# Fused retention attention and two MLPs on one core: first visits of 3, 7, 13 and 9 slices, and low parts a step later

## Chip, cores and metric

The kernel runs on one core of one Trainium2 chip. The metric is device time in microseconds of one execution; the kernel before has a median of 1159.39 us over three runs (1157.38 to 1161.65).

## What is computed

A linear attention with a decay for each head, and two pairs of dense layers behind it, the first with a leaky ReLU, the second with an ELU. Queries, keys and values are float32; **the weights are float64**.

```python
for t in range(S):                       # B 4, H 8, S 768, D 64
    state = gamma[None, :, None, None] * state + np.einsum('bhd,bhe->bhde', k[:, :, t], v[:, :, t])
    y[:, :, t] = scale * np.einsum('bhd,bhde->bhe', q[:, :, t], state)
x = y.transpose(0, 2, 1, 3).reshape(3072, 512)
h = x @ moe_w_in;  g = np.maximum(0.01 * h, h);  x = g @ moe_w_out      # 512 -> 2048 -> 512
h = x @ moe2_w_in; g = np.where(h > 0, h, np.exp(np.minimum(h, 0)) - 1); out = g @ moe2_w_out
```

## The kernel before

**Products.** Every operand of the dense layers is held as two float32r parts, high and low, and each product is three matmuls: high by high, high by low, low by high. Tokens go in six blocks of 512, the inner size of 2048 in 16 slices of 128. A **step** is one block with one slice: `gemm1` (L254) makes `h` with 12 matmuls, the first two of each three with the high part of the weights and the third with the low part; ACT makes `gf` (`leaky`, L343) and its high part `ghi`, DVE the low part `glo` (`split_g`, L266); `gemm2` (L273) then adds 12 matmuls into the four banks `y`. `drain` (L299) issues the gemm2 of the steps up to a given one, and at the end of a visit it evacuates `y` (two copies on DVE, two on ACT) to DRAM, or adds an earlier part.

**Weights.** A slice of first-phase weights comes in as raw 64-bit words, one MB for both of its matrices (`load`, L86, on SP's queue), and is turned into high and low parts on the chip, in place. The operations are listed once, in order, by `conv_ops` (L182): put (ACT takes the exponent words out), exp (two mask operations on DVE, then a bias on ACT), top, low and sign on DVE, mul on DVE with the copy w to the high part on ACT behind it, and split on DVE, the low part. The put of the next piece is issued between a piece's sign and its mul; the split of a piece comes after the exp of the next. The first slices are taken in halves (a: `w_in`, b: `w_out`), the others whole. `conv(n)` (L198) issues the next n of these, puts not counted, **as long as the piece at the head of the list has been asked for by `load`**; `need` (L211) issues as many as it takes to have a given slice ready.

**Order.** All engines work through their instructions in program order, and the program's order is written out by hand. First come chunks 0 to 7 of the attention (128 tokens each, for blocks 0 and 1; L483): for each, the scores of the next chunk, `prep` on POOL, the chunk's outputs, the next chunk's mask (`pt`, DVE), then one conversion operation, the new state and the low part of x, and one more conversion operation. Three pairs of PSUM banks rotate among scores and outputs. Then comes `plan` (L505), a list of (step, drain up to this step, operations before, operations after). An entry issues gemm1, `conv(n1)`, `gf`, `ghi` and `glo`, the drain, `conv(n2)` and possibly one `load_w`. Blocks 0 and 1 take turns in the first entries, so that one converted slice serves two steps; `VISITS` (L48) says how many slices each visit has. The other 16 chunks are spread over the steps (`out_at`, `sc_at`). The second phase takes its weights from DRAM, where the first phase's last visits leave them converted.

**Space.** Each slice has its tile `w0` to `w15`. Before raw words are put there, the upper ones hold the chunks' keys, queries and values (`kv`, chunk c in `w{15-c}`), the staged `y` of first visits (`w15`), and the `g` of steps that wait long for their gemm2 (`wait`, in `w14` and `w13`). A load into such a tile waits until it is free.

Of the kernel before, what the change touches and what calls it, by code (L numbers as in the profile page):

```python
# [20 lines left out]
F32 = mybir.dt.float32  # L21
F32R = mybir.dt.float32r
# [5 lines left out]
ALU = mybir.AluOpType  # L28
# [4 lines left out]
P = 128  # L33
C = 128
NT = B * S
NCB = S // C
NCH = B * NCB
NP = H // 2
BLK = 512
CPB = BLK // C  # L40
NB = NT // BLK
KD = DM // P
MF = DFF // P
HM = MF // 2
V0 = 4


VISITS = (  # L48
    [(0, 0, V0), (1, 0, HM), (0, V0, MF), (1, HM, MF)] + [(j, 0, MF) for j in range(2, NB)],
    [(j, 0, MF) for j in range(NB)],  # L50
)

# [2 lines left out]
def body(ctx: ExitStack, tc: tile.TileContext, kkv, w1, w2, tabs, out):  # L55
    nc = tc.nc
    big = ctx.enter_context(tc.tile_pool(name="big", bufs=1))
    wp = ctx.enter_context(tc.tile_pool(name="wp", bufs=1))
    cv = ctx.enter_context(tc.tile_pool(name="cv", bufs=2))
    gp = ctx.enter_context(tc.tile_pool(name="gp", bufs=2))  # L60
# [8 lines left out]
    xhi = [big.tile([P, KD, BLK], F32R, name=f"xhi{b}") for b in range(2)]  # L69
    xlo = [big.tile([P, KD, BLK], F32R, name=f"xlo{b}") for b in range(2)]  # L70
# [5 lines left out]
    nload = nload2 = 0  # L76


    halves = [(0, 0), (1, 0), (0, 1), (2, 0), (1, 1), (3, 0), (2, 1), (3, 1)]
    pieces = [(m, a, 1) for m, a in halves] + [(m, 0, 2) for m in range(V0, MF)]  # L80
    loaded = set()

# [15 lines left out]
    def load_w2():  # L98

        nonlocal nload2  # L100
        m = nload2
        for a in range(2) if m < V0 else (0,):
            n = 1 if m < V0 else 2
            t = place(m, a, n, F32R, "w")
# [91 lines left out]
    queue = list(conv_ops())  # L196

    def conv(n):  # L198

        while queue and queue[0][1][:2] in loaded:  # L200
            op, i = queue[0]
            if op is not c_put:
                if not n:
                    break
                n -= 1
            queue.pop(0)
            op(i)
            while exps:
                bias(exps.pop(0))
# [56 lines left out]
    def split_g(s, gf, eng, pool, bufs):  # L266
        ghi = pool.tile([P, BLK], F32R, tag="ghi", name="ghi", bufs=bufs)
        glo = pool.tile([P, BLK], F32R, tag="glo", name="glo", bufs=bufs)
        nc.scalar.copy(ghi, gf)  # L269
        eng.tensor_tensor(glo, gf, ghi.bitcast(F32), ALU.subtract)  # L270
        g[s] = ghi, glo
# [16 lines left out]
    acc, g = None, {}  # L288
# [54 lines left out]
    def leaky(h):  # L343
        gf = gp.tile([P, BLK], F32, tag="gf", name="gf", bufs=2)
        nc.scalar.activation(gf, h, AF.Prelu, alpha=0.01)  # L345
        return gf


    with ExitStack() as actx:
# [12 lines left out]
        def att_load(c, first=0, last=4):  # L362

            if first == 0:
                if c < 2 * CPB:
                    kv[c] = wp.tile([P, 4, DM], F32, tag=f"w{MF - 1 - c}", name="kv")
                else:
                    kv[c] = ap_.tile([P, 4, DM], F32, tag="kv", name="kv")
            nc.sync.dma_start(out=kv[c][:, first:last, :], in_=kkv[c, :, first:last, :])
# [31 lines left out]
        def outputs(c, pool, tag):  # L401


            cb = c % NCB
            t = pt.pop(c)
            o = pool.tile([P, 2, BLK], F32, tag=tag, name="o")
            places = [(i, k, 2 * i + k, r) for i in range(2) for k in range(2) for r in range(2)]
            by_column = [(i, k, 2 * i + k, x ^ k) for i in range(2) for k in range(2) for x in range(2)]
            for i, k, a, r in by_column:
                v = kv[c][:, 3, a * C + r * D : a * C + (r + 1) * D]  # L410
                nc.tensor.matmul(o[half(r ^ k), k, pair(i)], v, t[:, r, pair(a)], start=(i == 0), stop=True, skip_group_check=True)  # L411
            if cb < NCB - 1:
                for i, k, a, r in places:
                    hs = slice(a * C + r * D, a * C + (r + 1) * D)
                    nc.tensor.matmul(o[half(r), k, 2 * C + i * D : 2 * C + (i + 1) * D], kv[c][:, 2, hs], kv[c][:, 3, hs],  # L415
                                     start=False, stop=True, skip_group_check=True)
            if cb:
                for i, k, a, r in places:
                    nc.tensor.matmul(o[half(r ^ k), k, pair(i)], st[half(r), 2 * k + i, :], kv[c][half(r), 1, pair(a)],  # L419
                                     start=False, stop=True, skip_group_check=True)  # L420
            b, ts = c // CPB % 2, slice(c % CPB * C, (c % CPB + 1) * C)
            x = [z[b][:, :, ts].rearrange("p (k i) t -> p k i t", k=2) for z in (xhi, xlo)]
            y = o[:, :, : 2 * C].rearrange("p k (i t) -> p k i t", i=2)
            nc.scalar.copy(x[0], y)
            return o, x, y

        def states(c, o, x, y):
            cb = c % NCB
            if cb < NCB - 1:
                n = st.rearrange("p (k i) d -> p k (i d)", k=2)  # L430
                m = sg.rearrange("p (k i) d -> p k (i d)", k=2)
                if cb:
                    nc.vector.tensor_tensor(n, m, o[:, :, 2 * C : 2 * C + 2 * D], ALU.add)
                else:
                    nc.vector.tensor_copy(n, o[:, :, 2 * C : 2 * C + 2 * D])
            nc.vector.tensor_tensor(x[1], y, x[0].bitcast(F32), ALU.subtract)
            if cb < NCB - 2:
                nc.vector.tensor_tensor(sg, st, gtab.unsqueeze(2).to_broadcast([P, NP, D]), ALU.mult)

        def prep(c):  # L440
# [12 lines left out]
        for x in halves[2:]:  # L453
            load(*x, 1)
        nload = V0
        for _ in range(2):
            load_w()

        def warm(n):
# [10 lines left out]
        banks = itertools.cycle(((ps, "y0"), (ps, "y1"), (aps, "x")))  # L470

        def early_masked(c, sc):
            masked(c, sc, *((wp, "w7") if c % 2 else (ap_, "pt")))

        early_masked(0, scores(0, *next(banks)))
        o = outputs(0, *next(banks))
        warm(1)
        states(0, *o)
        sc = scores(1, *next(banks))
        prep(1)  # L480
        warm(1)
# [1 line left out]
        for c in range(1, 2 * CPB):  # L483
            if c + 1 < 2 * CPB:
                sc = scores(c + 1, *next(banks))
                prep(c + 1)
            o = outputs(c, *next(banks))
            if c + 1 < 2 * CPB:
                early_masked(c + 1, sc)
            conv(1)  # L490
            states(c, *o)
            conv(1)


        out_at, sc_at = {}, {}
# [5 lines left out]
        NA = next(s for s, (_, j, _, _) in enumerate(steps) if j == NB - 1)  # L501

        plan = [(0, -1, 2, 2), (4, -1, 2, 2), (1, 0, 4, 3), (5, 0, 2, 2), (2, 1, 4, 3), (6, 1, 2, 2), (3, 3, 2, 3), (7, 5, 3, 5)]  # L505
        plan += [(s, s - 2, 3 if s < 12 else 2, 3 if s == 8 else 2) for s in range(8, NA)]
        wait = [wp.tile([P, 4, BLK], F32R, tag=f"w{MF - 2 - i}", name="gx") for i in range(2)]
        for n, (s, upto, n1, n2) in enumerate(plan):
            ph, j, m, (_, _, m0, m1, vi) = steps[s]
            h = (aps if n % 2 else ps).tile([P, BLK], F32, tag="z" if n % 2 else "h", name="h")  # L510
            gemm1(0, m, j % 2, h)
            conv(n1)
            gf = leaky(h)
            c = out_at.get(s)
            if c is not None:
                o = outputs(c, aps, "x")
                states(c, *o)
                if c < NCH - 2:
                    att_load(c + 2)
            if 4 <= s < 8:  # L520
                i = 2 * (s % 2)
                ghi, glo = g[s] = [wait[s // 2 - 2][:, i + k, :] for k in range(2)]
                nc.scalar.copy(ghi, gf)
                nc.vector.tensor_tensor(glo, gf, ghi.bitcast(F32), ALU.subtract)
            else:
                split_g(s, gf, nc.vector, gp, 3)
            drain(upto, stage_w if vi < 2 or m < m0 + 2 and vi == 2 else stage_f)
            c = sc_at.get(s)
            if c is not None:
                sc = scores(c, aps, "x")  # L530
                prep(c)
                masked(c, sc, ap_, "pt")
            conv(n2)
            if s in (8, 9):
                att_load(2 * CPB + s - 8)
            if nload < (MF - 1 if s > 11 else MF - 3) or vi > 1 and m > m0 + 1:
                load_w()
            if vi > 3:

                if m == 2 and npre < 2 * MF:  # L540
                    pre_load()
                if 2 < m < MF - 1:
                    pre(m < MF - 2)
            if m0 > 0 and m == m1 - 3:
                need(MF - 1, 1)
                reload(0, j, stage_f)


    with ExitStack() as ectx:
# [44 lines left out]
        for s in range(NA, 2 * NS):  # L594
# [6 lines left out]
            if ph == 0:  # L601
                gf = leaky(h)
# [10 lines left out]
            if (ph, vi) in comes:  # L613
                nx, i = comes[ph, vi], m // 2
# [68 lines left out]
```

## Time and profile before

| | |
|---|---|
| median of three runs | 1159.39 us |
| the profiled execution | 1159.4 us, its span 1157.6 us |
| PE busy | 1138.3 us of the span |
| DVE, ACT, POOL busy | 653.2, 542.2 and 93.2 us |
| mean granted TensorE clock | 0.995 |
| HBM read, written | 84.68 and 31.46 MB |

The span runs from the first to the last instruction of the profiled execution. Busy times are sums over an engine's instructions. Matmuls are pipelined, so one of them lasts longer (0.39 us) than the distance to the next (0.227 us); a group of 12 is best read from start to start. A timeline row's bracket says how long the engine stood idle ahead of it and what released it. A line number can be that of a helper: L176 is every split, L172 every w, L270 every `glo`.

### The profile page before, as it was taken

The page shows a single profiled execution, that of the slowest core. Times are in us where ns is not written, and L with a number is a line of the kernel's source. Part 1 is how long each engine was busy: PE and PEld are TensorE (multiplying, and loading weights), DVE is VectorE, ACT ScalarE, POOL GpSimd, SP SyncE. Part 2 cuts the span into 40 slices and gives each one's busy share as a digit, 9 for nine tenths or more (in the row PEclk, how much of TensorE's full clock was granted, in tenths as well). Part 3 has the DMA queues.
Part 4 walks back from the last instruction along what each step waited for, and adds up shares of the span by engine and source line. Part 5 has one row for each costly group of instructions (what it writes and reads, how often), then busy time and mean ns, then how long its engine had stood idle before and what let it go on. Part 6 is the DMA issues. An engine that isn't in the chain of part 4 may idle for free.

```text
span 1157.6 us, 14906 instructions
## 1 busy us (share of the span) xinstructions
PE 1138.3 (98%) x6024; PEld 930.9 (80%) x6024; DVE 653.2 (56%) x1049; ACT 542.2 (47%) x901; POOL 93.2 (8%) x77
## 2 busy tenths in 40 slices
PE   8989999999999999999999999999999999999998
PEld 6767788788888888888888888888888888888886
DVE  5879773235654564651212666666666666766655
ACT  2555552224444443441323654654654655555553
POOL 4000001102221222220000000000000000000000
PEclk9989999999999999999999999999999999999999
DMA  9931303334554554430645400100100100000000
GB/s 377 377 129 54 109 21 116 115 115 154 193 200 154 193 195 151 161 131 1 218 183 196 148 19 1 55 19 1 55 19 1 55 19 1 37 1 1 37 1 37
DMA packets 29877, 117.10 MB, mean 101 GB/s; under 512 B 3312, under 2 KB 3312, under 8 KB 23792
## 3 DMA queue, kind: packets, MB, share of 16 engines
q1 hardware_dynamic: 29808, 116.15, 27.4%
q8 instruction: 47, 0.77, 0.3%
q14 instruction: 22, 0.18, 0.1%
HBM read 84.68 MB, written 31.46 MB: 100 GB/s over the span
## 4 chain that ended last, share of the span: by engine, by line
PE 89%; DVE 4%; ACT 2%; issue 0%; ACTq 0%; DVEq 0%
PE y L286 43%; PE h L263 42%; PE sc L393 2%; PE o L411 1%; DVE f L134 1%; DVE f L127 1%; PE o L419 1%; ACT w L172 1%; PE o L415 1%; ACT e L120 0%; DVE glo L270 0%; DVE e L131 0%; DVE f L123 0%; DVE w L176 0%; ACT gf L345 0%; ACT ghi L269 0%
## 5 line engine op out<-in xcount | busy, mean ns | idle before, releaser
L263 PE MATMUL h<-xhi,w 128*128 128x512 f32 x1536 | 506.2, 391 | 1.8 <-DVE w L176 1.2
L270 DVE TENSOR_TENSOR glo<-gf,ghi 128x512 fp32r<-128x512 f32 x188 | 131.0, 697 | 375.6 <-ACT ghi L269 373.6
L263 PEld LDWEIGHTS h<-xhi,w 128*128 128x128 f32 x1536 | 288.0, 188 | 65.6 <-DVE w L176 2.5
L263 PE MATMUL h<-xlo,w 128*128 128x512 f32 x768 | 299.0, 389 | 0.0
L286 PE MATMUL y<-ghi,w 128*128 128x512 f32 x736 | 247.3, 398 | 5.7 <-DVE w L176 2.4
L286 PE MATMUL y<-w,ghi 128*128 128x512 f32 x768 | 236.5, 389 | 0.0
L286 PEld LDWEIGHTS y<-ghi,w 128*128 128x128 f32 x736 | 140.1, 191 | 38.6 <-DVE w L176 2.9
L286 PEld LDWEIGHTS y<-w,ghi 128*128 128x128 f32 x768 | 144.1, 188 | 29.9
L263 PEld LDWEIGHTS h<-xlo,w 128*128 128x128 f32 x768 | 144.3, 188 | 29.5
L572 ACT ACTIVATE n<-h 128x512 f32<-128x512 f32 x96 | 57.4, 598 | 224.3 <-PE h L263 224.3
L286 PE MATMUL y<-w,glo 128*128 128x512 f32 x384 | 149.4, 389 | 0.0
L286 PE MATMUL y<-glo,w 128*128 128x512 f32 x368 | 144.7, 393 | 0.0
L345 ACT ACTIVATE gf<-h 128x512 f32<-128x512 f32 x96 | 56.9, 593 | 164.4 <-PE h L263 164.1
L269 ACT CAST ghi<-gf 128x512 fp32r<-128x512 f32 x188 | 115.3, 613 | 5.8 <-DVE gf L583 3.4
L286 PEld LDWEIGHTS y<-w,glo 128*128 128x128 f32 x384 | 72.1, 188 | 15.0
L286 PEld LDWEIGHTS y<-glo,w 128*128 128x128 f32 x368 | 70.3, 191 | 14.4
L580 DVE SCALAR_TENSOR_TENSOR a<-n,a 128x512 f32<-128x512 f32 x96 | 65.6, 684 | 5.9 <-ACT n L575 5.9
L582 DVE SCALAR_TENSOR_TENSOR t<-a,t 128x512 f32<-128x512 f32 x96 | 66.4, 692 | 3.3
L583 DVE SCALAR_TENSOR_TENSOR gf<-h,t 128x512 f32<-128x512 f32 x96 | 66.4, 691 | 3.3
L120 ACT ACTIVATE e<-e,ebias 128x512 int16<-128x512 uint16 (+1 forms) x52 | 42.7, 821 | 50.9 <-DVE e L117 50.9
L581 DVE SCALAR_TENSOR_TENSOR t<-n,t 128x512 f32<-128x512 f32 x96 | 65.7, 685 | 0.0
L573 ACT ACTIVATE t<-n 128x512 f32<-128x512 f32 x96 | 60.7, 632 | 3.1
(51 smaller groups left out, 806.3 us busy)
## 6 DMA issues: line engine op xcount, KB each, us to landing
kv<-in_kkv SPq DMA_DIRECT2D x23, 1024.0 KB, 6.2
raw<-in_w SPq DMA_DIRECT2D x40, 512.0 KB, 3.8
wscr<-raw SPq DMA_DIRECT2D x32, 512.0 KB, 2.6
raw<-in_w SPq DMA_DIRECT2D x12, 1024.0 KB, 11.5
w<-wscr SPq DMA_DIRECT2D x12, 1024.0 KB, 4.7
xs<-yscr SPq DMA_DIRECT2D x12, 512.0 KB, 3.7
out<-osb SPq DMA_DIRECT2D x24, 256.0 KB, 2.9
yscr<-ysb SPq DMA_DIRECT2D x16, 256.0 KB, 2.8
```

Of the source, the lines that this page charges most:

```text
L120: nc.scalar.activation(e.bitcast(I16), e, AF.Relu, bias=ebias, scale=2.0**3)
L263: nc.tensor.matmul(h, a, x, start=(n == 0), stop=(n == 3 * KD - 1))
L269: nc.scalar.copy(ghi, gf)
L270: eng.tensor_tensor(glo, gf, ghi.bitcast(F32), ALU.subtract)
L286: nc.tensor.matmul(acc[d], lhsT, rhs, start=(first and n == 0), stop=(last and n == 2))
L345: nc.scalar.activation(gf, h, AF.Prelu, alpha=0.01)
L572: nc.scalar.activation(n, h, AF.Relu, scale=-1.0)
L573: nc.scalar.activation(t, n, AF.Tanh, scale=-0.5)
L580: nc.vector.scalar_tensor_tensor(out=a, in0=n, scalar=1.0, in1=a, op0=ALU.add, op1=ALU.mult)
L581: nc.vector.scalar_tensor_tensor(out=t, in0=n, scalar=1.0, in1=t, op0=ALU.add, op1=ALU.mult)
L582: nc.vector.scalar_tensor_tensor(out=t, in0=a, scalar=2.0, in1=t, op0=ALU.add, op1=ALU.mult)
L583: nc.vector.scalar_tensor_tensor(out=gf, in0=h, scalar=0.0, in1=t, op0=ALU.max, op1=ALU.add)
```

## The change

The first visits have 3 and 7 slices where they had 4 and 8 (`V0, V1 = 3, 7`), so slices 0 to 2 come in halves, and seven slices are used by both blocks in turn. `plan` is written anew. The `g` of eight steps (3, 4, 5, 10 to 13) waits in four tiles, `w14` down to `w11`, where four steps' waited in two. Three slices are asked for ahead of the plan, then one for each entry up to 11 slices; the other five are asked for from entry 16 on. `glo` is written in the next entry, behind its `conv(n1)`, unless the drain of its own entry wants it or nothing is left to convert. In the attention, DVE's new state comes ahead of ACT's copy of the output, and the low part of x (with the decayed state) an iteration later in the first eight chunks, behind the next mask. In chunks 4 to 7 one conversion operation is issued and not two.

```diff
-HM = MF // 2
-V0 = 4
+V0, V1 = 3, 7
-    [(0, 0, V0), (1, 0, HM), (0, V0, MF), (1, HM, MF)] + [(j, 0, MF) for j in range(2, NB)],
+    [(0, 0, V0), (1, 0, V1), (0, V0, MF), (1, V1, MF)] + [(j, 0, MF) for j in range(2, NB)],
...
-    halves = [(0, 0), (1, 0), (0, 1), (2, 0), (1, 1), (3, 0), (2, 1), (3, 1)]
+    halves = [(0, 0), (1, 0), (0, 1), (2, 0), (1, 1), (2, 1)]
...
-            nc.scalar.copy(x[0], y)
-            return o, x, y
-
-        def states(c, o, x, y):
+            return o
+
+        def states(c, o):
...
                     nc.vector.tensor_copy(n, o[:, :, 2 * C : 2 * C + 2 * D])
+            x, y = halves_of(c, o)
+            nc.scalar.copy(x[0], y)
...
+        def lows(c, o):
+
+            x, y = halves_of(c, o)
             nc.vector.tensor_tensor(x[1], y, x[0].bitcast(F32), ALU.subtract)
-            if cb < NCB - 2:
+            if c % NCB < NCB - 2:
                 nc.vector.tensor_tensor(sg, st, gtab.unsqueeze(2).to_broadcast([P, NP, D]), ALU.mult)
...
-        for _ in range(2):
+        for _ in range(3):
             load_w()
...
-            o = outputs(c, *next(banks))
+            before, o = o, outputs(c, *next(banks))
             if c + 1 < 2 * CPB:
                 early_masked(c + 1, sc)
+            lows(c - 1, before)
             conv(1)
-            states(c, *o)
-            conv(1)
+            states(c, o)
+            if c < CPB:
+                conv(1)
+        lows(c, o)
...
-        plan = [(0, -1, 2, 2), (4, -1, 2, 2), (1, 0, 4, 3), (5, 0, 2, 2), (2, 1, 4, 3), (6, 1, 2, 2), (3, 3, 2, 3), (7, 5, 3, 5)]
-        plan += [(s, s - 2, 3 if s < 12 else 2, 3 if s == 8 else 2) for s in range(8, NA)]
-        wait = [wp.tile([P, 4, BLK], F32R, tag=f"w{MF - 2 - i}", name="gx") for i in range(2)]
+        plan = [(0, -1, 2, 2), (3, -1, 2, 2), (1, 0, 2, 4), (4, 0, 2, 2), (2, 1, 3, 3), (5, 5, 0, 5)]
+        plan += [(6, 5, 2, 2), (10, 5, 2, 2), (7, 6, 2, 3), (11, 6, 2, 2), (8, 7, 2, 3), (12, 7, 2, 2), (9, 9, 1, 4), (13, 12, 3, 6)]
+        plan += [(s, s - 2, 3, 2) for s in range(14, NA)]
+        later = {}
+        for k, (m, ss) in enumerate(((MF - 2, (3, 4)), (MF - 3, (5,)), (MF - 4, (10, 11)), (MF - 5, (12, 13)))):
+            t = wp.tile([P, 4, BLK], F32R, tag=f"w{m}", name="gx")
+            later.update({x: (t[:, 2 * i, :], t[:, 2 * i + 1, :]) for i, x in enumerate(ss)})
+        lows_due = []
+
+        def g_lows():
+            while lows_due:
+                s, gf = lows_due.pop()
+                nc.vector.tensor_tensor(g[s][1], gf, g[s][0].bitcast(F32), ALU.subtract)
+
         for n, (s, upto, n1, n2) in enumerate(plan):
...
             conv(n1)
+            g_lows()
             gf = leaky(h)
...
+            nc.scalar.copy(g[s][0], gf)
+            lows_due.append((s, gf))
+            if not queue or s <= upto:
+                g_lows()
...
-            if s in (8, 9):
-                att_load(2 * CPB + s - 8)
-            if nload < (MF - 1 if s > 11 else MF - 3) or vi > 1 and m > m0 + 1:
+            if s in (14, 15):
+                att_load(2 * CPB + s - 14)
+            if nload < (MF if n > 15 else MF - 5):
                 load_w()
```

## Rows read from the trace of the kernel before

**Rows 1.** The page's first part: busy us (share of the span) and instructions.
```profile
PE 1138.3 (98%) x6024; PEld 930.9 (80%) x6024; DVE 653.2 (56%) x1049; ACT 542.2 (47%) x901; POOL 93.2 (8%) x77
```

**Rows 2.** Busy time by stretch: columns named in the first line.
```profile
core 0: us, PE busy (x) PEld busy (x) DVE busy (x) ACT busy (x) POOL busy (x), PEclk, DMA share, GB/s
...
28.00:38.30 10.30, 6.89 (x136) 5.77 (x133) 10.23 (x18) 3.55 (x6) 2.85 (x2) 1.00 1.02 422
...
68.05:76.00 7.95, 7.95 (x22) 6.34 (x23) 5.05 (x10) 2.51 (x4) 0.00 (x0) 0.62 0.01 2
...
90.00:102.50 12.50, 11.54 (x49) 8.42 (x47) 11.66 (x17) 7.91 (x11) 0.00 (x0) 1.00 0.22 84
...
122.50:129.30 6.80, 4.62 (x14) 3.57 (x14) 5.98 (x9) 4.38 (x7) 0.00 (x0) 0.75 0.69 201
```

**Rows 3.** Timeline of PE: start us, us, instruction; in brackets idle before, and releaser.
```profile
36.24 1.09 PE L411 MATMUL o<-pt,kv 128*64 128x128 f32 x16 [1.59 <-DVE pt L399]
...
38.33 0.50 PE L263 MATMUL h<-xhi,w 128*128 128x512 f32 x1
...
64.89 0.50 PE L286 MATMUL y<-ghi,w 128*128 128x512 f32 x1 [1.14 <-ACT w L172]
...
68.05 1.22 PE L286 MATMUL y<-ghi,w 128*128 128x512 f32 x2 [2.42 <-DVE w L176]
...
124.81 0.47 PE L286 MATMUL y<-ghi,w 128*128 128x512 f32 x1 [2.18 <-DVE ysb L320]
...
129.22 0.40 PE L263 MATMUL h<-xhi,w 128*128 128x512 f32 x1
...
183.83 0.67 PE L419 MATMUL o<-kv,st 64*64 64x128 f32 x16
```

**Rows 4.** Chain that ended last, in order of time: start us, us.
```profile
132.13 2.72 PE y L286 x12
```

**Rows 5.** Timeline of DVE, then of POOL, in the first chunks.
```profile
26.91 1.13 DVE L116 TENSOR_SCALAR s<-e 128x512 uint16<-128x512 uint16 x1
...
29.41 1.22 DVE L176 TENSOR_TENSOR w<-f,w 128x512 fp32r<-128x512 f32 x1
...
29.05 1.05 POOL L375 TENSOR_TENSOR kv<-kv,tab 128x512 f32<-128x512 f32 x1 [1.16 <-DMA kv<-in_kkv]
```

**Rows 6.** Timeline of DVE: one half piece, from split to split.
```profile
49.52 0.69 DVE L176 TENSOR_TENSOR w<-f,w 128x512 fp32r<-128x512 f32 x1 [0.16 <-ACT w L172]
...
51.28 0.69 DVE L270 TENSOR_TENSOR glo<-gf,ghi 128x512 fp32r<-128x512 f32 x1 [0.74 <-ACT ghi L269]
...
54.33 0.69 DVE L176 TENSOR_TENSOR w<-f,w 128x512 fp32r<-128x512 f32 x1 [0.16 <-ACT w L172]
```

**Rows 7.** Timeline of DVE: one whole slice, from split to split.
```profile
95.80 1.22 DVE L176 TENSOR_TENSOR w<-f,w 128x1024 fp32r<-128x1024 f32 x1 [0.32 <-ACT w L172]
...
98.80 0.69 DVE L270 TENSOR_TENSOR glo<-gf,ghi 128x512 fp32r<-128x512 f32 x1
...
102.46 1.23 DVE L176 TENSOR_TENSOR w<-f,w 128x1024 fp32r<-128x1024 f32 x1 [0.32 <-ACT w L172]
```

**Rows 8.** Timeline of ACT: `gf`, `ghi`, a put, the next; and a w.
```profile
65.38 0.58 ACT L345 ACTIVATE gf<-h 128x512 f32<-128x512 f32 x1
66.05 0.62 ACT L523 CAST gx<-gf 128x512 fp32r<-128x512 f32 x1
66.57 1.11 ACT L113 COPY e<-raw 128x1024 int16<-128x1024 int16 x1
67.58 0.59 ACT L345 ACTIVATE gf<-h 128x512 f32<-128x512 f32 x1
...
101.38 1.05 ACT L172 CAST w<-f 128x1024 fp32r<-128x1024 f32 x1 [2.40 <-DVE f L134]
```

**Rows 9.** DMA issues in 95 to 103 us: KB each, median us to landing.
```profile
raw<-in_w SPq DMA_DIRECT2D x1, 1024.0 KB, 4.7
```

**Rows 10.** Timeline of DVE: the state of the first later chunk.
```profile
185.19 0.42 DVE L433 TENSOR_TENSOR st<-sg,o 128x256 f32<-128x256 f32 x1 [4.45 <-ACT xhi L424]
```

More of the change, by code (lines that the diff above doesn't have):

```diff
@@ L420, in outputs @@
                                      start=False, stop=True, skip_group_check=True)
-            b, ts = c // CPB % 2, slice(c % CPB * C, (c % CPB + 1) * C)
-            x = [z[b][:, :, ts].rearrange("p (k i) t -> p k i t", k=2) for z in (xhi, xlo)]
-            y = o[:, :, : 2 * C].rearrange("p k (i t) -> p k i t", i=2)
-            nc.scalar.copy(x[0], y)
-            return o, x, y
-        def states(c, o, x, y):
+            return o
+        def states(c, o):
             cb = c % NCB
@@ L435, in states, with halves_of @@
                     nc.vector.tensor_copy(n, o[:, :, 2 * C : 2 * C + 2 * D])
+            x, y = halves_of(c, o)
+            nc.scalar.copy(x[0], y)
+        def halves_of(c, o):
+            b, ts = c // CPB % 2, slice(c % CPB * C, (c % CPB + 1) * C)
+            x = [z[b][:, :, ts].rearrange("p (k i) t -> p k i t", k=2) for z in (xhi, xlo)]
+            return x, o[:, :, : 2 * C].rearrange("p k (i t) -> p k i t", i=2)
+        def lows(c, o):
+            x, y = halves_of(c, o)
             nc.vector.tensor_tensor(x[1], y, x[0].bitcast(F32), ALU.subtract)
-            if cb < NCB - 2:
+            if c % NCB < NCB - 2:
                 nc.vector.tensor_tensor(sg, st, gtab.unsqueeze(2).to_broadcast([P, NP, D]), ALU.mult)
@@ L477, in body @@
         warm(1)
-        states(0, *o)
+        states(0, o)
         sc = scores(1, *next(banks))
@@ L516, in body @@
                 o = outputs(c, aps, "x")
-                states(c, *o)
+                states(c, o)
+                lows(c, o)
                 if c < NCH - 2:
                     att_load(c + 2)
[L520 to L524, printed above, removed]
-            else:
-                split_g(s, gf, nc.vector, gp, 3)
+            if s in later:
+                g[s] = later[s]
+            else:
+                g[s] = [gp.tile([P, BLK], F32R, tag=x, name=x, bufs=3) for x in ("ghi", "glo")]
+            nc.scalar.copy(g[s][0], gf)
+            lows_due.append((s, gf))
+            if not queue or s <= upto:
+                g_lows()
             drain(upto, stage_w if vi < 2 or m < m0 + 2 and vi == 2 else stage_f)
```

## The prediction, made before the changed kernel was run

> **What bounds the kernel now.** I read the page's engine busy times first, then the chain that ended last, then busy time by stretch, and last the timelines of PE, DVE and ACT over the first 180 us. PE is busy for 98% of the span [rows 1], and from about 130 us on the chain is matmul groups end to end, 2.72 us for each group of 12 [rows 4]; the change leaves that part's matmuls as they are. What can move is the start and the stretch in which the weights are converted. Call the gemm1 of a step g1, its gemm2 g2, and T0 the start of the first g1: 38.33 us [rows 3]. From T0 to 129.22 us PE runs 28 such groups, 76.2 us of work, in 90.9 us: **14.7 us are lost**. They lie in three places. The first is the wait for the output half of slice 2 (64.9 to 68.05, with 1.14 and 2.42 us idle) and the slow clock behind it: at a granted 0.62, 22 matmuls take 7.95 us instead of 5.0 [rows 2, 3]; about 7.6 in all. The second is three waits for `w L176` from 90 to 106 us, about 1 us each, where the clock stays at full speed, 2.9 in all [rows 2]. The third is the first visit's evacuation, 2.18 us idle and again a slow clock, 4.0 in all [rows 2, 3]. Behind all three stands DVE, in part because it waits in every step for ACT's `ghi` before it can write `glo` (0.74 us in the row) [rows 6]. Before T0, in 28 to 38.3 us, DVE is full (10.23 of 10.3) and PE works 6.9 of 10.3 us [rows 2].
>
> **The start.** Chunk 7's outputs wait for its `pt` on DVE, which sits behind everything DVE was given before [rows 3]. Ahead of that `pt` now stand two conversion operations fewer (low and sign of m1a) and one low part of x fewer (chunk 5's); at about 0.6 us each, 0.8 for the sign, that is 2.0 us. Not all of it arrives: the bank in which chunk 7's scores are put is now freed by the low part of chunk 4, which comes after chunk 6's `pt`, and the bank of chunk 7's outputs by that of chunk 5, after chunk 7's own `pt`. Walking DVE's new order from the same first operation, with the same durations, sets T0 to 37.7 where the two operations that were slow in the trace (1.13 and 1.22 us, beside POOL's `kv` [rows 5]) are slow again, and to 36.4 where neither is; a split of this size took 0.69 later [rows 6]. I take 37.4, **0.9 us gained**. Ends: nothing, and 4.8 us, where only the last chunk's arrival (POOL's wait for it ended at 29.05 [rows 5]) and 4.5 us of scores, mask and outputs behind it count. The Trainium skill, "SBUF — State Buffer", section "Who interferes with whom", says that DVE and GpSimd share one port pair, which a DVE operation of certain modes or with two SBUF inputs cannot share; the two slow rows agree, and by it T0 would be the 37.7.
>
> **States first.** In the trace `st` waits for ACT's copy from the same bank [rows 10]. Putting `st` first turns this around: ACT's copy now waits for 0.4 us of DVE. None of the 16 later chunks shows a PE wait at the products with `st` (the first of them stands in [rows 3]), so this is worth nothing to PE after the start; if ACT's next copy became late it would cost up to 0.4 us for each chunk, which the two steps between a step's g1 and its g2 cover.
>
> **What conversion costs.** A half piece needs 3.3 us of DVE: split to split is 4.81, less waits of 0.74 and 0.16 and a `glo` of 0.61 [rows 6]. A whole slice needs 5.73: 6.66 less 0.32 and 0.61 [rows 7]. Two blocks at once give PE 10.9 us for each slice, so DVE (5.73 and two `glo`) has room; one block gives 5.44 us, and DVE (6.3) has none. The order decides the rest, and ACT's above all: from the end of a g1, `gf` takes 0.67 to the next start, `ghi` 0.52, a whole slice's put 1.01, and w 1.05 [rows 8], then the split 1.22 [rows 7]. A put and w written behind a step's `gf` so free the next split 3.25 us after that g1 ended, and PE's third matmul (the first to read low parts) at 4.55.
>
> **Losses after the change**, from T0, in PE groups. (a) Up to g2 of step 2, DVE has 27 operations (4.5 half pieces, 15 us), six `glo` and chunk 7's low part, 20 us against PE's eight groups, 21.8: in time. But plan entry (5, 5, 0, 5) wants the `glo` of step 5 in its own step, and it is written ahead of the mul, exp and split of the output half of slice 2. So after the g1 of step 5 (21.8) come `gf`, `ghi`, `glo`, mul and w: 25.1, PE idle for **3.3**; the split ends at 25.9, another **0.4**. Gaps of 2.18 us and more were followed by a slow clock, at 1.7 us (12 matmuls in 4.4 us) to 3.0 us [rows 2, 3]; I take **2.3**. The evacuation of block 0's first visit then hides behind this slow g2. (b) Step 6 follows with a put and w behind its `gf`; only step 10's g1 lies between it and step 7's, so that one's third matmul waits from 3.17 to 4.55: **1.4**. (c) DVE starts exp of m5 at 43.6 and owes 23 operations (22 us) and seven `glo` (4.3 us) up to the `glo` of step 9: 70 us. PE wants the `glo` of step 8 at 64.7 and gets it at 66.4, and that of step 9 at 69.3 and gets it at 70.1: **2.7** with restarts; ends 0 and 4. (d) load_w stops at 11 slices until plan entry 16. `conv` takes nothing from the queue whose raw slice has not been asked for, and the put of m11 stands ahead of the mul of m10: entries 14 to 16 convert nothing, though DVE has the time. The tile of m11 also holds g of step 13 until that g2 ends, two steps (5.4 us) before m10 is wanted. The load takes 4.7 us [rows 9]; put, w and split behind it free the third matmul at 8.3 where PE wants it at 5.9: **2.4**. If the load takes 2 us longer, 4.4. (e) Steps 18 to 21 then have each put, w and split between one g1 and the next: PE wants the third matmul at 3.17 and gets it at 4.55, with the restart **1.5 each, 6.0**. DVE's own 6.3 us fit in the 6.95 that a step then takes. (f) Step 22: **0.7**, as everything left of m15 is forced at entry 20. After it nothing waits, as now. The sum is 6.0 + 1.4 + 2.7 + 2.4 + 6.0 + 0.7 = **19.2 us against 14.7**.
>
> **DMA and queues.** The deferred loads pass SP behind two `kv` loads that have no wait; all five are freed with m11's tile, so m12 to m15 land in time. Low parts a step later cost no operation; their cover is that g2 comes two entries behind g1, and it is gone in entries (5, 5) and (9, 9), which (a) and (c) count.
>
> **The sum.** 1159.4 (the profiled execution; the median is 1159.39, so no correction) − 0.9 + 19.2 − 14.7 = **1163.0 us**. A measurement of this kernel can tell about 0.5% from no change: faster is below 1153.6, slower above 1165.2.
>
> **Rivals.** *The clock falls at step 17* (slower). Forecast (d) has PE idle for 1.6 us and then 0.8. The trace's longest gap without a slow clock is 1.59 us and its shortest with one is 2.18 [rows 3]: if the load takes over 0.6 us longer than 4.7, this gap passes 2.18, and 1.7 to 3.0 us come on top of the longer gap: 1163.0 + 1.5 + 2.3 = 1167. Against it: nothing else is on the DMA queue then. *The last slices don't bind* (faster). If conversion were far enough ahead that (d), (e) and (f) vanish, 9.1 us go: 1154, and with (c) gone too 1151. For it: seven doubled slices give DVE time. Against it: the load count in the plan stops the queue whatever time DVE has. *The low parts really come free* (a change that does what it says): without the wait in (a) 6.0 us go, 1157; against it stands the order written out in that entry.
>
> **Chances.** The forecast, with the third rival and the ends of the start and of (c), lies within 0.5%: 0.60. The clock at step 17, or (a) and (c) at their dear ends: 0.28. The last slices free: 0.12. The range runs from 1155 (start at 35, (a) gone or (d) to (f) mostly gone) to 1170 (clock, a late load, no gain at the start).
>
> **What would show it.** T0 near 37.4. One gap of about 3.3 us at g2 of step 2, then a granted clock near 0.6. No conversion on DVE for some 10 us ahead of step 17, a gap there, and then five g1 with a wait for `w L176` about 7 us apart. The forecast is wrong if those five show no wait, if DVE converts through entries 14 to 16, or if PE never loses its clock at step 2.

## The result, and the profile after

The changed kernel takes **1168.1 us** (median; 1166.9 to 1169.6) against 1158.5 for the kernel before in the same rounds: a ratio of 1.0079, 95% interval 1.0055 to 1.0103, 9.6 us slower. The forecast was 1163.0 with a range of 1155 to 1170, and "slower by over 0.5%" had a chance of 0.28; that is the case that came. The profiled execution is the fastest of the changed kernel's, 1166.9 us with a span of 1165.1, 7.5 us over the span before.

Its page shows PE with the same work (answers to [rows 1]):

```profile
span 1165.1 us, 14891 instructions
PE 1138.6 (98%) x6024; PEld 927.8 (80%) x6024; DVE 652.6 (56%) x1042; ACT 542.5 (47%) x898; POOL 92.5 (8%) x77
```

Busy time by stretch in the changed kernel, as in [rows 2] (columns: stretch and us; busy us and instructions of PE, PEld, DVE, ACT, POOL; granted clock, DMA share, GB/s):

```profile
28.00:39.50 11.50, 9.39 (x191) 8.13 (x187) 9.88 (x15) 3.64 (x7) 4.42 (x4) 1.00 1.02 426
...
62.00:65.40 3.40, 0.04 (x1) 0.00 (x0) 1.95 (x4) 1.83 (x3) 0.00 (x0) 1.00 0.00 0
65.40:77.20 11.80, 11.77 (x49) 9.14 (x50) 10.05 (x14) 5.37 (x6) 0.00 (x0) 1.00 0.28 90
...
102.00:109.00 7.00, 4.95 (x20) 3.41 (x20) 6.25 (x10) 5.37 (x7) 0.00 (x0) 1.00 0.00 0
...
130.50:138.80 8.30, 6.21 (x28) 4.50 (x26) 2.60 (x5) 4.41 (x5) 0.00 (x0) 1.00 0.80 301
138.80:143.00 4.20, 4.20 (x12) 3.33 (x13) 4.09 (x5) 0.05 (x1) 0.00 (x0) 0.59 1.01 425
143.00:172.00 29.00, 24.61 (x100) 17.80 (x99) 23.93 (x31) 17.25 (x20) 0.00 (x0) 1.00 0.14 51
```

The gaps themselves stand in PE's timeline of the changed kernel, as in [rows 3]. L410 is a chunk's outputs, L392 its scores, L262 a g1, L285 a g2; L443 is the low part of x, L175 a split, L171 a w, L527 a `glo`:

```profile
16.65 1.09 PE L410 MATMUL o<-pt,kv 128*64 128x128 f32 x16 [1.92 <-DVE xlo L443]
...
26.57 1.16 PE L392 MATMUL sc<-kv 64*128 64x128 f32 x16 [1.41 <-issue]
...
31.07 1.16 PE L392 MATMUL sc<-kv 64*128 64x128 f32 x16 [1.25 <-issue]
...
37.36 1.09 PE L410 MATMUL o<-pt,kv 128*64 128x128 f32 x16 [0.52 <-DVE xlo L443]
...
39.44 0.50 PE L262 MATMUL h<-xhi,w 128*128 128x512 f32 x1
...
65.41 0.50 PE L285 MATMUL y<-ghi,w 128*128 128x512 f32 x1 [3.37 <-ACT w L171]
...
83.19 0.50 PE L262 MATMUL h<-xhi,w 128*128 128x512 f32 x1 [0.57 <-ACT w L171]
...
84.45 0.73 PE L262 MATMUL h<-xhi,w 128*128 128x512 f32 x2 [0.53 <-DVE w L175]
...
105.01 0.50 PE L285 MATMUL y<-glo,w 128*128 128x512 f32 x1 [1.45 <-DVE glo L527]
...
108.69 0.50 PE L285 MATMUL y<-glo,w 128*128 128x512 f32 x1 [0.60 <-DVE glo L527]
...
137.52 0.50 PE L262 MATMUL h<-xhi,w 128*128 128x512 f32 x1 [1.56 <-ACT w L171]
...
138.78 1.10 PE L262 MATMUL h<-xhi,w 128*128 128x512 f32 x2 [0.53 <-DVE w L175]
...
146.21 0.50 PE L262 MATMUL h<-xhi,w 128*128 128x512 f32 x1 [0.55 <-ACT w L171]
...
147.47 0.73 PE L262 MATMUL h<-xhi,w 128*128 128x512 f32 x2 [0.52 <-DVE w L175]
```

And the chain that ended last (start us, us) shows steps 17 and 18 being made to wait: the load of m11, then put, w and split, then PE:

```profile
130.59 4.82 DMA raw<-in_w
...
135.43 1.09 ACT e L112
136.52 0.96 ACT w L171
...
137.50 1.24 DVE w L175
...
138.78 4.15 PE h L262 x10
...
142.95 0.61 ACT gf L344
...
143.59 0.62 ACT ghi L547
144.21 1.00 ACT e L112
145.21 0.96 ACT w L171
...
146.19 1.23 DVE w L175
...
147.47 2.59 PE h L262 x10
```

Read from the starts of PE's groups, less 2.72 us for each, what is lost after T0 is:

| term | forecast | in the profile |
|---|---|---|
| T0 (38.33 before) | 37.4 | 39.44 |
| up to the g1 of step 5 | 0 | 0.7 |
| (a) g2 of step 2 | 6.0 | 4.3 |
| (b) steps 6 to 7 | 1.4 | 1.7 |
| (c) g2 of steps 8 and 9 | 2.7 | 2.7 |
| (d) step 17 | 2.4 | 4.2 |
| (e) steps 18 to 21 | 6.0 | 6.8 |
| (f) step 22 | 0.7 | 0.7 |
| sum after T0 (14.7 before) | 19.2 | 21.1 |

T0 is 1.1 us later and 6.4 us more are lost after it: the 7.5 us of the spans. The rest of the 9.6 is the difference between these two executions and their medians (1.2 and 0.9 us).

### The profile page after: what moved, and what is told of

Same layout as the page of the kernel before. It is cut to its first block, busy times and chain, and to the rows that moved or that the text cites. A ratio compares the mean times of both kernels' runs of the same rounds, so it can differ in the third digit from the quotient of the medians.

```text
span 1165.1 us, 14891 instructions
## 1 busy us (share of the span) xinstructions
PE 1138.6 (98%) x6024; PEld 927.8 (80%) x6024; DVE 652.6 (56%) x1042; ACT 542.5 (47%) x898; POOL 92.5 (8%) x77
## 4 chain that ended last, share of the span: by engine, by line
PE 92%; DVE 3%; ACT 2%; DMA 1%; issue 1%; SPq 0%; ACTq 0%; DVEq 0%
PE h L262 43%; PE y L285 43%; PE sc L392 2%; PE o L410 2%; DVE w L175 1%; PE o L418 1%; DMA kv<-in_kkv 1%; ACT w L171 1%; PE o L414 1%; ACT e L112 1%; DVE f L133 0%; DVE f L126 0%; DMA raw<-in_w 0%; ACT gf L344 0%; DVE e L130 0%
## 5 line engine op out<-in xcount | busy, mean ns | idle before, releaser
L262 PE MATMUL h<-xhi,w 128*128 128x512 f32 x1536 | 507.6, 392 | 7.9 <-ACT w L171 4.4
L262 PEld LDWEIGHTS h<-xhi,w 128*128 128x128 f32 x1536 | 288.4, 188 | 74.7 <-ACT w L171 7.0
L262 PE MATMUL h<-xlo,w 128*128 128x512 f32 x768 | 299.6, 390 | 0.0
L285 PE MATMUL y<-ghi,w 128*128 128x512 f32 x712 | 236.2, 393 | 3.4 <-ACT w L171 3.4
L285 PE MATMUL y<-w,ghi 128*128 128x512 f32 x768 | 236.4, 389 | 0.0
L262 PEld LDWEIGHTS h<-xlo,w 128*128 128x128 f32 x768 | 144.7, 188 | 29.5
L285 PEld LDWEIGHTS y<-w,ghi 128*128 128x128 f32 x768 | 144.1, 188 | 29.8
L285 PEld LDWEIGHTS y<-ghi,w 128*128 128x128 f32 x712 | 133.4, 188 | 35.1 <-ACT w L171 3.8
L285 PE MATMUL y<-w,glo 128*128 128x512 f32 x384 | 149.4, 389 | 0.0
L285 PE MATMUL y<-glo,w 128*128 128x512 f32 x356 | 138.8, 390 | 2.0 <-DVE glo L527 2.0
L527 DVE TENSOR_TENSOR glo<-gf,ghi 128x512 fp32r<-128x512 f32 x73 | 51.2, 703 | 120.7 <-ACT ghi L547 120.7
L285 PEld LDWEIGHTS y<-w,glo 128*128 128x128 f32 x384 | 72.1, 188 | 15.1
L285 PEld LDWEIGHTS y<-glo,w 128*128 128x128 f32 x356 | 66.8, 188 | 16.2 <-DVE glo L527 2.8
L268 ACT CAST ghi<-gf 128x512 fp32r<-128x512 f32 x112 | 68.0, 607 | 3.9 <-DVE gf L607 3.4
L119 ACT ACTIVATE e<-e,ebias 128x512 int16<-128x512 uint16 (+1 forms) x51 | 42.4, 831 | 42.8 <-DVE e L116 42.8
```

What stands on the lines that cost most here:

```text
L119: nc.scalar.activation(e.bitcast(I16), e, AF.Relu, bias=ebias, scale=2.0**3)
L262: nc.tensor.matmul(h, a, x, start=(n == 0), stop=(n == 3 * KD - 1))
L285: nc.tensor.matmul(acc[d], lhsT, rhs, start=(first and n == 0), stop=(last and n == 2))
L527: nc.vector.tensor_tensor(g[s][1], gf, g[s][0].bitcast(F32), ALU.subtract)
```

## The experiments

**Where does the load count bind?** The waiting `g` (of seven steps, 3 to 5 and 10 to 13; "eight" in the text on the change is a miscount) is put under other slices, and the last five slices are asked for earlier.

```diff
-        for k, (m, ss) in enumerate(((MF - 2, (3, 4)), (MF - 3, (5,)), (MF - 4, (10, 11)), (MF - 5, (12, 13)))):
+        for k, (m, ss) in enumerate(((MF - 5, (3, 4)), (MF - 4, (5,)), (MF - 3, (10, 11)), (MF - 2, (12, 13)))):
...
-            if nload < (MF if n > 15 else MF - 5):
+            if nload < (MF - 5 if n < 6 else MF - 3 if n < 13 else MF - 2 if n < 15 else MF):
```

> The changed kernel with one thing put otherwise: the g that waits sits so that the slices asked for first find free tiles (m11 and m12 under steps 3 to 5, m13 under 10 and 11, m14 under 12 and 13), and slices 11 and 12 are asked for from entry 6 on, 13 from entry 13, 14 and 15 from entry 15. Theory (the load count in the plan stops the conversion queue): DVE converts through entries 14 to 16, the five gaps from step 17 on go, and with them 9.1 us and the slow clock behind the first: 1157 to 1159 us where the changed kernel has 1168. Rival (DVE has no room there anyway, 6.3 us of work for each 5.44 us of PE): the gaps stay, at about 0.9 us for each of six slices, and 4 to 5 us are gained: 1163 to 1164.

Measured: 1159.1 us, ratio to the kernel before 1.000 (0.999 to 1.0011), **9.0 us less than the changed kernel**. Busy time by stretch in this kernel:

```profile
62.00:78.00 16.00, 12.67 (x48) 9.64 (x47) 11.38 (x17) 7.18 (x9) 0.00 (x0) 0.89 0.19 67
...
130.00:145.00 15.00, 13.61 (x59) 10.64 (x58) 14.47 (x19) 9.41 (x12) 0.56 (x1) 1.00 0.45 175
145.00:160.00 15.00, 15.00 (x68) 12.43 (x67) 14.47 (x20) 9.34 (x12) 0.00 (x0) 1.00 0.12 34
```

PE has no idle time from 145 us on, and DVE converts through: the theory holds. DVE's lack of room shows only as 1.19 and 0.21 us at two g2 between 130 and 138 us. The first line is worth a look too: at the same gap at step 2 (3.32 us here, 3.37 there) the clock fell in this execution and stayed at full speed in the changed kernel's.

**The first chunks.** The low part of x comes right behind the state again.

```diff
         states(0, o)
+        lows(0, o)
...
-            before, o = o, outputs(c, *next(banks))
+            o = outputs(c, *next(banks))
...
-            lows(c - 1, before)
             conv(1)
             states(c, o)
+            lows(c, o)
             if c < CPB:
                 conv(1)
-        lows(c, o)
```

> The changed kernel with the low part of x and the decayed state right behind the new state in the first eight chunks, as before the change; the state stays ahead of ACT's copy and chunks 4 to 7 keep their one conversion operation. Theory (a bank of outputs stays taken until a low part that now comes behind the next mask): the gaps ahead of scores and outputs go, the first gemm1 begins at about 37 us and not at 39.4, and the time falls by 2 us to 1166. Rival (DVE operations slowed beside POOL set the start): the first gemm1 stays at 39 us or later and the time at 1168.

Measured: 1167.1 us, ratio 1.0073 (1.0061 to 1.0086), T0 at 38.16: 1.0 us less, inside the interval of the changed kernel, so by itself inconclusive. T0 of one execution is a weak witness: kernels with the very start of the changed one began at 39.23, 39.44, 40.73 and 40.91, those with this start at 38.16, 38.18 and 39.95. In the two latest of the first four the clock fell behind the 1.92 us gap that all four have ahead of chunk 1's outputs; these are the changed kernel's row and that of the kernel with earlier loads (T0 40.73):

```profile
16.00:21.00 5.00, 4.35 (x90) 3.99 (x92) 3.23 (x7) 1.31 (x2) 2.15 (x3) 1.00 1.02 423
...
16.00:21.00 5.00, 4.60 (x64) 4.14 (x64) 1.93 (x6) 1.31 (x2) 1.04 (x1) 0.66 1.01 418
```

In the profile with 39.95, four DVE operations that overlap POOL's `kv` took 1.13 to 1.80 us each, where the same lines took 0.28 to 0.68 when nothing slowed them. So the reverse was run too, the new order alone in the kernel before (both conversion operations left in place):

```diff
-            nc.scalar.copy(x[0], y)
-            return o, x, y
...
+            return o
...
+            x, y = halves_of(c, o)
+            nc.scalar.copy(x[0], y)
...
-            o = outputs(c, *next(banks))
+            before, o = o, outputs(c, *next(banks))
...
+            lows(c - 1, before)
             conv(1)
-            states(c, *o)
+            states(c, o)
             conv(1)
+        lows(c, o)
```

> The kernel before with the new order of the first eight chunks alone: the state ahead of ACT's copy, the low part of x and the decayed state an iteration later; both conversion operations of each chunk stay where they were. Theory (banks stay taken by outputs whose low part comes later): gaps ahead of scores as in the changed kernel, the first gemm1 at 40 to 41 us and not at 38.3, and 1160.5 to 1162. Rival (what made the start late in the changed kernel is when the chunks arrive, not the order): the first gemm1 within 0.7 us of 38.3 and the time at 1159.

Measured: 1161.1 us, ratio 1.0016 (1.0006 to 1.0026): **the new order costs 2.0 us by itself**, and the gaps of the changed kernel (1.92, 1.40, 1.25 and 0.52 us) are there again, ahead of the same scores and outputs. The theory holds. Its T0 of 41.99 has a slow clock in it too, a granted 0.57 from 8 to 12 us and 0.73 from 16 to 21 us; how much of the 2.0 us comes by the gaps themselves, and how much by the clock behind them, was not separated.

**Entry (5, 5, 0, 5).**

```diff
-        plan = [(0, -1, 2, 2), (3, -1, 2, 2), (1, 0, 2, 4), (4, 0, 2, 2), (2, 1, 3, 3), (5, 5, 0, 5)]
+        plan = [(0, -1, 2, 2), (3, -1, 2, 2), (1, 0, 2, 4), (4, 0, 2, 2), (2, 1, 3, 6), (5, 5, 0, 5)]
```

> The changed kernel with plan entry (2, 1, 3, 3) as (2, 1, 3, 6): mul, exp and split of the output half of slice 2 are issued an entry earlier, ahead of step 5's low part. Theory (the order in that entry makes the wait): the gap of 3.4 us ahead of the gemm2 of step 2 falls under 0.7 us, and a slow clock behind it, where there is one, goes too: 3 to 5 us less, 1163 to 1165. Rival (DVE is late there whatever the order): the wait moves to step 5's low part or to the evacuation and no more than 1 us is gained: 1167.

Measured: 1164.9 us, ratio 1.0048 (1.0034 to 1.0062), **3.2 us less**. In its PE timeline 0.60 us are left of the 3.37, now waiting for the evacuation:

```profile
66.81 8.45 PE L285 MATMUL y<-gx,w 128*128 128x512 f32 x36 [0.60 <-DVE ysb L319]
```

**The three edits together**, loads, first chunks and entry (2, 1, 3, 6), with no further one.

```diff
+        lows(0, o)
...
-            lows(c - 1, before)
...
+            lows(c, o)
...
-        plan = [(0, -1, 2, 2), (3, -1, 2, 2), (1, 0, 2, 4), (4, 0, 2, 2), (2, 1, 3, 3), (5, 5, 0, 5)]
+        plan = [(0, -1, 2, 2), (3, -1, 2, 2), (1, 0, 2, 4), (4, 0, 2, 2), (2, 1, 3, 6), (5, 5, 0, 5)]
...
-            if nload < (MF if n > 15 else MF - 5):
+            if nload < (MF - 5 if n < 6 else MF - 3 if n < 13 else MF - 2 if n < 15 else MF):
```

> The three edits together: earlier loads, low parts of x at once in the first chunks, and the earlier split for step 2. Theory: they add up, 9 to 11 + 2 + 3 to 5 us: 1150 to 1154, which is below the kernel before too. Rival (what is won early is lost again to DVE between steps 6 and 13): the gaps ahead of the gemm2 of steps 8 and 9 grow by what was won, and the time is 1155 to 1159.

Measured: 1153.2 us, ratio 0.9953 (0.9940 to 0.9967). They add up, and to a little more: 14.9 us less than the changed kernel, where one by one they gave 9.0, 1.0 and 3.2. What the rival named did not grow: 1.46 and 0.65 us ahead of the g2 of steps 8 and 9.

**More of m4 ahead of step 6**, in the kernel with the three edits.

```diff
-        plan = [(0, -1, 2, 2), (3, -1, 2, 2), (1, 0, 2, 4), (4, 0, 2, 2), (2, 1, 3, 6), (5, 5, 0, 5)]
+        plan = [(0, -1, 2, 2), (3, -1, 2, 2), (1, 0, 2, 4), (4, 0, 2, 2), (2, 1, 3, 6), (5, 5, 0, 9)]
```

> The three edits together, with plan entry (5, 5, 0, 5) as (5, 5, 0, 9) besides: the put of m5 and all of m4 but its mul are issued ahead of step 6's gf. Theory (that put and w stand behind a gf that waits for PE, so DVE idles 4 to 5 us, and lacks them from step 7 to step 9): the wait ahead of step 7's gemm1 goes (1.4 us), the gaps ahead of the gemm2 of steps 8 and 9 shrink to under 0.5 us together, and 3 to 4 us are gained against 1153.2: 1149 to 1150. Rival (DVE loses in between what it gains): only step 7's wait goes, 1152.

Measured: 1154.0 us, ratio 0.9958 (0.9944 to 0.9971): nothing gained. Step 7's wait is gone, as both expected, but PE's timeline has new ones:

```profile
90.00 0.50 PE L285 MATMUL y<-glo,w 128*128 128x512 f32 x1 [0.90 <-DVE glo L527]
...
99.34 0.50 PE L285 MATMUL y<-glo,w 128*128 128x512 f32 x1 [0.77 <-DVE glo L527]
...
103.79 0.50 PE L285 MATMUL y<-ghi,w 128*128 128x512 f32 x1 [1.64 <-ACT ghi L547]
...
124.65 2.79 PE L285 MATMUL y<-gx,w 128*128 128x512 f32 x11 [0.76 <-DVE gx L527]
```

All but one wait for a low part (`glo`, or `gx` where it lies in a `w` tile): DVE is bound in this stretch (11.45 of 12 us in 90 to 102). The edit fills the pause with four conversion operations but takes none out of the entries behind it, so DVE starts the exp of m5 3.8 us earlier after T0 (35.6 against 39.4) and then has 28.6 us of work, not 25.4, up to the end of step 9's `glo`, which comes at 66.3 us after T0 against 65.8. The run so cannot tell the pause from the sum of the work; the rival, that DVE loses in between what it gains, is the nearer.

**Low parts of g an entry later, alone.** In the kernel before, with its own visits, plan, loads and chunks:

```diff
             conv(n1)
+            g_lows()
             gf = leaky(h)
...
-                nc.scalar.copy(ghi, gf)
-                nc.vector.tensor_tensor(glo, gf, ghi.bitcast(F32), ALU.subtract)
...
-                split_g(s, gf, nc.vector, gp, 3)
...
+            nc.scalar.copy(g[s][0], gf)
+            lows_due.append((s, gf))
+            if not queue or s <= upto:
+                g_lows()
```

> The kernel before with one part of the change: the low part of g an entry later, behind that entry's conversion operations, unless the entry's own drain wants it; visits, plan, loads and attention as before. Theory (DVE and ACT wait for each other in every step, and DVE comes late to the output half of slice 2 and to the evacuation by what it waits): the 6.4 us that DVE waits for ghi up to 67 us go, the gap at slice 2 shrinks to under 1 us and its slow clock with it, the evacuation's gap to about 1 us: 1150 to 1153 us. Rival (DVE is bound by its own work there): the waits reappear as waits for w and no more than 3 us are gained: 1156 to 1159.

Measured: **1147.7 us, ratio 0.9902 (0.9886 to 0.9917): 11.4 us faster than the kernel before** and 20.5 faster than the changed one. After T0, PE's timeline has two gaps left:

```profile
67.29 0.50 PE L286 MATMUL y<-ghi,w 128*128 128x512 f32 x1 [0.60 <-ACT w L172]
...
96.54 0.73 PE L263 MATMUL h<-xhi,w 128*128 128x512 f32 x2 [0.53 <-DVE w L176]
```

The waits at slice 2 and at the evacuation and the slow clock behind both ([rows 2, 3]) are gone; more than the theory asked for. Of the 14.7 us lost after T0, 2.7 are left. DVE's waits for ACT's high part from 38 to 132 us (us in total, times, longest), in the kernel before and in this one:

```profile
DVE glo L270 <- ACT ghi L269: 6.4, 6, 2.3
DVE gx L524 <- ACT gx L523: 4.8, 4, 2.0
...
DVE glo L513 <- ACT ghi L533: 1.2, 1, 1.2
```

That is 11.2 us in ten waits before, and 1.2 in one now. (The expectation's 6.4 us are the first of these rows, up to 132 us; up to 67 us both rows together have 5.6.) The reverse, the changed kernel with every low part in its own entry:

```diff
-            if not queue or s <= upto:
-                g_lows()
+            g_lows()
```

> The changed kernel with every low part of g in its own entry, as before the change; visits, plan, loads and start are those of the change. Theory (the deferral is the part that wins, here too): DVE waits for ghi again in each entry while it converts, some 0.75 us in 10 to 13 entries and 0.5 us in each of steps 17 to 21: 1174 to 1180. Rival (with the load count stopping the queue, DVE has time to wait): 1167 to 1170, no difference that can be told.

Measured: 1189.6 us, ratio 1.0262 (1.0242 to 1.0282), 21.5 us slower than the changed kernel. Right in direction, far too small in size. DVE's waits from 38 to 180 us:

```profile
DVE glo L527 <- ACT ghi L547: 27.5, 12, 5.1
DVE gx L527 <- ACT gx L547: 9.3, 5, 3.5
```

That is 36.8 us in 17 waits, on average over 2 us each where 0.75 had been put down; the changed kernel has 10.3 us in 4 such waits there. PE itself stands 3.21 us for ACT's `ghi` at one g2, and its granted clock is 0.79 to 0.91 in six of the ten stretches from 38 to 200 us.

**The start on top of the best**, in the kernel of the 1147.7 us:

```diff
-            states(c, *o)
-            conv(1)
+            states(c, o)
+            lows(c, o)
+            if c < CPB:
+                conv(1)
...
-        plan = [(0, -1, 2, 2), (4, -1, 2, 2), (1, 0, 4, 3), (5, 0, 2, 2), (2, 1, 4, 3), (6, 1, 2, 2), (3, 3, 2, 3), (7, 5, 3, 5)]
+        plan = [(0, -1, 2, 2), (4, -1, 2, 2), (1, 0, 4, 3), (5, 0, 2, 2), (2, 1, 4, 3), (6, 1, 2, 2), (3, 3, 5, 3), (7, 5, 3, 5)]
```

> The kernel before with the low part of g an entry later (1147.7 us by itself), and two small edits: in the first eight chunks the state comes ahead of ACT's copy, low parts of x at once, one conversion operation and not two in chunks 4 to 7; and plan entry (3, 3, 2, 3) as (3, 3, 5, 3). Theory (the start is DVE's sum up to the last mask, and DVE has the time for four operations later, now that it no longer waits): the first gemm1 comes about 1.3 us earlier and nothing new waits: 1146 to 1147. Rival (the four operations are what DVE lacks later): the gap at slice 3 and the wait of about 90 us grow by 2 us: 1148 to 1150.

Measured: 1149.0 us, ratio 0.9909 (0.9894 to 0.9923), not better than the kernel without these edits, and rather a little slower (1148.8 to 1149.3 against 1147.2 to 1148.1). T0 comes 1.1 us earlier (38.09 against 39.19), as the theory had it, but the gap at slice 3 is 1.41 us where it was 0.60, and of PE's time after T0 2.2 us more are lost: the rival holds.

## Why the prediction was right and where it was wrong

**Right: the direction, (b), (c), (e), (f), and the idle part of (a) and (d).** The gaps lie at the steps that were named, with the releasers that were named: 3.37 us at step 2 (3.3), 1.56 and 0.53 at step 17 (1.6 and 0.8), then one g1 each 7.1 us (6.95) with split last, and DVE without conversion ahead of step 17 but for one mul (from 124.4 to 136.5 us). Two of these, (a) and the load count of (d) to (f), were taken away singly and gave 3.2 and 9.0 us, so they are shown as causes. (c) fits the account that was given for it: DVE starts the exp of m5 42.8 us after T0 (43.6) and ends the `glo` of step 9 at 69.2 (70.1), with hardly a pause in between (the third busy time is DVE's):

```profile
82.22:108.63 26.41, 23.32 (x99) 17.97 (x97) 25.40 (x34) 19.21 (x24) 0.00 (x0) 1.00 0.00 1
```

That is agreement and no test: no run took work away from DVE in this stretch, or put the `glo` of steps 8 and 9 ahead of conversion. In (e) the 4.55 us are 4.47 by the terms given, 3.25 and 1.22; a step then lost 1.7 us and not 1.5.

**Luck in the sum.** The 19.2 us forecast and the 21.1 measured are near each other in part because two errors cancel: the slow clock that was put at step 2 did not come there (1.7 us too much in (a)), and one that was not in the sum came at step 17 (1.8 us too little in (d)). Of the 5.1 us between forecast and median, 2.0 are the start, 1.9 the losses after T0, and 1.2 the distance of the profiled execution from the median.

**Wrong: the start.** The step "Not all of it arrives" names the banks of chunk 7 only. The same rule, a bank is free only when the low part that reads it is done, holds up chunk 1's outputs (1.92 us) and the scores of chunks 5 and 6 (1.41 and 1.25): each waits for a low part that now follows the next mask. Two of the rows carry "issue" as their releaser; DVE's timeline of the changed kernel shows what it was, two low parts of x that end 0.1 us before the scores begin:

```profile
23.41 1.32 DVE L130 TENSOR_TENSOR e<-e,s 128x512 uint16<-128x512 uint16 x1
...
25.79 0.67 DVE L443 TENSOR_TENSOR xlo<-o,xhi 128x512 fp32r<-128x512 f32 x1
...
27.97 1.27 DVE L116 TENSOR_SCALAR e<-e 128x512 uint16<-128x512 uint16 x1
...
30.29 0.68 DVE L443 TENSOR_TENSOR xlo<-o,xhi 128x512 fp32r<-128x512 f32 x1
```

The other two rows belong to it: these operations took 0.42 and 0.29 us elsewhere (at 39.74 and 17.16), and here they ran while POOL worked on `kv` (from 23.16 and 27.81, 1.28 us each). That puts the two low parts behind by 0.9 and 1.0 us, and the two are as slow at the same places in all five profiles with the new order. The prediction walked with two slow operations as well, but with those of the trace before (T0 37.7). T0 went 1.1 us up and not 0.9 down, and the reversed experiment puts the price of the order, with these operations in it, at 2.0 us.

**Wrong: the clock.** The step that set 1.59 and 2.18 us as the gaps without and with a slow clock took one execution for a rule. In the changed kernel's profile the 3.37 us at step 2 left the clock at full speed, where 2.3 us had been put down, and step 17's gaps of 1.56 and 0.53 were followed by a granted clock of 0.59 (10 matmuls in 4.15 us and not 2.3). The rival of the slow clock at step 17 came true without the late load it was tied to: the load took 4.82 us. In the profiles of the experiments on the first chunks and on entry (5, 5, 0, 5), with 2.03 and 1.71 us idle at step 17, the clock fell there too (0.89 over 130 to 145 us), and at step 2, behind gaps of 3.32 and 3.37 us, it fell in the profiles of the earlier loads and of the first chunks (0.89 over 62 to 78 us) and not in the changed kernel's. The changed kernel's other three executions have a lower mean granted clock (0.994 to 0.996 against 0.998), so a slow clock at step 2 may be what sets the median above the profiled execution; no trace shows it.

**Missed: what the parts are worth.** The low parts of g were given no price of their own; they only entered the walk of (a) and (c). Alone they take 11.4 us off, and the other parts, beside them, put 20.5 us back: 14.9 by the load count, entry (5, 5, 0, 5) and the start, and 5.5 between the kernel without these three (1153.2) and the low parts alone (1147.7). (Parts are not worth the same everywhere: in the changed kernel the low parts are worth 21.5.) Of these 5.5 the gaps in PE's timeline account for 4, and in the two profiles T0 for another 0.8: the kernel of the 1153.2 us has 1.1 us at step 7, 0.55 at the evacuation, 2.1 at the g2 of steps 8 and 9 and 1.35 at later ones, 5.1 in all, where the low parts alone leave 1.1. Which part of the new plan (visits, drains or conversion counts) makes these was not tried one by one and stays open; the one count that was tried moved them without gain. The third rival, low parts that come free, was priced at 6 us by the one gap at step 2; the trace had the larger sum in view, in DVE's ten waits for the high part, of which [rows 6] has one of 0.74 us, 11.2 us in all, and in the slow clock behind PE's two long gaps.

## What to carry to other kernels

Price each part of a change by itself, also where the sum comes out near zero: a good part of 11 us and bad parts of 20 us look like a small loss. Where two engines wait for each other once in each step, try moving the later half of the exchange one step back: here it paid 11.4 us, though a single wait was only 0.36 to 2.27 us, as nine of ten such waits went and with them the two gaps of PE that had brought a slow clock (4.6 us of the 14.7, from [rows 2, 3]). A list that is worked off in order stops at the first entry whose data has not been asked for, so ask for data where the list needs it, not where a tile happens to be free, and place what must wait in the tiles that are needed last.

## What the runs showed of the chip

The granted clock after a gap is not a matter of the gap's length alone: 3.37 us of idle PE left it at full speed in one execution, 3.32 us at the same place brought 0.89 over 16 us in another, and 1.56 and 0.53 us, 0.7 us apart, brought 0.59 over the next 4.2 us. The 1.92 us ahead of chunk 1's outputs left it at 1.00 in two profiles and brought 0.66 over 16 to 21 us in two others of the same start, whose first g1 came 1.3 to 1.7 us later. And a DVE operation that meets POOL's work on `kv` can take three to four times as long: 1.27 us for 0.29, 1.32 for 0.42.
